# The first block's attention by token tile, with two heads on alternate partitions among zeros

## The chip, the cores and the metric

The kernel runs on one core of a Trainium2 chip. The metric is the device time of one execution in microseconds. Engines are PE (TensorE), DVE (VectorE), ACT (ScalarE), POOL (GpSimd) and SP (SyncE, which here only issues loads and stores). Each takes its instructions in the order of the program, and waits are on semaphores.

## The reference

4 batches of 768 tokens, 8 heads of 64. Attention is by chunks of 32 queries: each sees 8 memory rows and the keys from 16 ahead of the chunk to 8 behind it, 64 in all. The 3072 x 512 result goes through a rational function between two matrices, and then through a soft mixture of experts:

```python
scores = scale * np.matmul(q_c, k_full.transpose(0, 1, 3, 2))   # per chunk of 32 queries
a = np.exp(scores - max);  a = a / (a.sum() + 1e-9);  x = a @ v_full
h = x @ w_in                                                      # 512 -> 2048
P = a[0] + a[1]*h + a[2]*h**2 + a[3]*h**3
Q = 1.0 + abs(b[0])*abs(h) + abs(b[1])*h**2
y = (P / (Q + 1e-6)) @ w_out                                      # 2048 -> 512
logits = y @ phi      # soft mixture: softmax over tokens and over slots, 8 experts of 4 slots
```

w_in and w_out come as float64 and are narrowed to float32 on the chip.

## The kernel before

3072 tokens are worked off in six blocks of 512 (four token tiles of 128). A block has eight steps; step i makes 256 columns of h (`h_part`, L380: on PE, x turned times w_in), then the rational function (`a1`, L607 to L610 on ACT and L609 on DVE; `d1`, L619 and L620; `a2`, L624 and L625; `t`, L632 and L633), then `post` turns the result and adds its logits (L398, L405, L406). h has two buffers in PSUM, so h of the next step runs on PE while ACT and DVE work on this one.

Attention is a generator, `attention(pair)`, for two tiles at once. Its steps: scores (L168; 64 products of 64 x 32 x 64, a head and a chunk each, two heads on the two halves of the partitions), maximum and difference (L186, L189, DVE), exp (L190, ACT), transposes (L208, PE), copy (L212, ACT), sums and reciprocal (L197 to L199, DVE), the product with v (L228, 64 products), scaling (L238, DVE), transposes (L246, PE) and copy to x (L250, ACT). The pairs of the later blocks run in pieces (`at`) between the steps of the block before. The first block has none ahead of it: its two pairs A and B run at the start, in an order written out by hand in `KN['pre']`, one letter for the next piece of a generator (A, B; s, t and n narrow weights; c makes constants; fN are N idle products on PE, L288). That order is kept as it stands on PE, ACT, DVE and POOL. `KN['loads']` is the order of loads on SP; SP lets a load go when the eighth load before it has landed.

In block 0 the weights come in. For each step 1 MB of w_in (`load_w_in`, L317) and 1 MB of the turned w_out (`load_w_turned`, L323) go through four staging buffers `g`; `f64_narrow` makes float32 of them: L303 and L305 on ACT, L304 and L307 on DVE, for each of the two. `wp_sum` (L483 to L489) multiplies w_out by phi. `KN['ord0']` lists what step kk of block 0 issues: `s2` narrows w_in two steps ahead, `i4` loads it four ahead, `o3` loads the turned w_out three ahead, `n1` narrows it one ahead, `z0` multiplies it by phi. Within the steps a scheduler orders the instructions of an engine.

## Time and profile before

| | |
|---|---|
| median of 3 runs | 577.13 us (575.4 to 579.71) |
| the profiled execution | 577.91 us, span 575.8 us |
| busy of the span | PE 540.6 us (94%), DVE 456.3 (79%), ACT 427.9 (74%), POOL 122.2 (21%) |
| HBM | 94.44 MB read, 182 GB/s over the span |
| chain that ended last | PE 56%, DVE 15%, ACT 14%, DMA 8%, issue 4% |

The share of busy time is an average over stages with different limits: at the start the engines wait for loads and for each other, in block 0 the weights are narrowed beside the steps, later PE has three products for each of block 0's.

### The profile page before, as it was taken

The numbers are of one execution on the slowest core, as the hardware profiler recorded it, in microseconds if no ns is written. First come the engines' busy times: TensorE is split into PE (matmuls) and PEld (weight loads), VectorE is DVE, ScalarE is ACT, GpSimd is POOL, SyncE is SP. The second block draws the span as 40 slices with busy tenths as digits, with TensorE's granted clock in tenths as the row PEclk, the third lists the DMA queues.
The fourth block names the chain that finished last, engine by engine and source line by source line (L and its number), as shares of the span: only waits on it lengthen the run. The fifth ranks groups of instructions, "written<-read, shape, count | busy, mean of one in ns | idle before, by whom it ended". The sixth has DMA issues, their size and how long they took to land.

```text
span 575.8 us, 13647 instructions
## 1 busy us (share of the span) xinstructions
PE 540.6 (94%) x5874; PEld 362.1 (63%) x5874; DVE 456.3 (79%) x572; ACT 427.9 (74%) x551; POOL 122.2 (21%) x66
## 2 busy tenths in 40 slices
PE   6799897999999999999999999999999999999991
PEld 6644443557767767677766777776768767643351
DVE  3759988989898999979899799898898978831042
ACT  1489896897978999779787888896888978721132
POOL 0001111213221322313231313132223322300000
PEclk8799898999999999999999999999999999999996
DMA  8997854301125315341432335304349374799948
GB/s 319 361 382 256 279 189 162 137 12 56 56 76 183 129 56 183 115 170 36 161 111 74 114 107 184 110 12 174 110 145 372 106 252 150 268 392 410 409 173 357
DMA packets 28139, 105.80 MB, mean 184 GB/s; under 512 B 3376, under 2 KB 3504, under 8 KB 27056
## 3 DMA queue, kind: packets, MB, share of 16 engines
q1 hardware_dynamic: 26928, 100.74, 48.1%
q0 software_dynamic: 1152, 4.19, 1.8%
q8 instruction: 46, 0.75, 0.5%
q14 instruction: 13, 0.11, 0.0%
HBM read 94.44 MB, written 10.49 MB: 182 GB/s over the span
## 4 chain that ended last, share of the span: by engine, by line
PE 56%; DVE 15%; ACT 14%; DMA 8%; issue 4%; POOL 1%; ACTq 0%; SPq 0%; DVEq 0%; POOLq 0%
PE h L380 28%; DMA g<-in_w_turned_dram 5%; PE m L405 4%; PE m L458 4%; ACT S L607 3%; PE lg L398 3%; ACT S L608 3%; ACT g L406 3%; DVE T L619 3%; PE h L796 2%; PE m L228 2%; DVE T L620 2%; PE lg L833 2%; DMA g<-in_moe_w_in_dram 2%; DVE T L632 2%
## 5 line engine op out<-in xcount | busy, mean ns | idle before, releaser
L380 PE MATMUL h<-xt,win 128*128 128x512 f32 x1012 | 268.5, 414 | 0.7 <-DVE T L620 0.6
L380 PEld LDWEIGHTS h<-xt,win 128*128 128x128 f32 x1012 | 184.1, 188 | 50.9 <-issue 12.3
L585 POOL TENSOR_TENSOR S<-S,S 128x1024 f32<-128x1024 f32 x46 | 112.2, 2440 | 335.1 <-DVE S L609 282.1
L607 ACT ACTIVATE S<-h,ctab 128x1024 f32<-128x1024 f32 x47 | 52.5, 1117 | 38.3 <-PE h L380 37.5
L609 DVE SCALAR_TENSOR_TENSOR S<-S,S 128x1024 f32<-128x1024 f32 x47 | 57.3, 1220 | 24.3 <-ACT S L608 23.7
L619 DVE TENSOR_TENSOR T<-T,h 128x1024 f32<-128x1024 f32 x47 | 57.1, 1215 | 7.6 <-ACT T L610 7.6
L405 PEld LDWEIGHTS m<-ident,T 128*128 128x128 f32 x384 | 43.4, 141 | 29.4 <-issue 14.0
L620 DVE SCALAR_TENSOR_TENSOR T<-T,ctab,h 128x1024 f32<-128x1024 f32 x47 | 59.9, 1274 | 0.7
L632 DVE SCALAR_TENSOR_TENSOR T<-T,ctab,S 128x1024 f32<-128x1024 f32 x46 | 58.6, 1274 | 0.0
L633 DVE SCALAR_TENSOR_TENSOR T<-S,T 128x1024 f32<-128x1024 f32 x46 | 56.1, 1220 | 2.4 <-DVE T L632 0.5
L406 ACT ACTIVATE g<-m 128x512 f32<-128x512 f32 x96 | 53.2, 601 | 6.3 <-PE m L405 6.0
L610 ACT ACTIVATE T<-h,ctab 128x1024 f32<-128x1024 f32 x47 | 57.5, 1223 | 0.0
L625 ACT ACTIVATE S<-S,ctab 128x1024 f32<-128x1024 f32 x47 | 54.5, 1159 | 0.9
L624 ACT ACTIVATE S<-S 128x1024 f32<-128x1024 f32 x47 | 50.5, 1074 | 6.1 <-DVE S L609 6.1
L405 PE MATMUL m<-ident,T 128*128 128x128 f32 x384 | 53.0, 278 | 1.2 <-DVE a L189 1.2
L608 ACT ACTIVATE S<-h,ctab 128x1024 f32<-128x1024 f32 x47 | 52.7, 1121 | 0.9 <-DVE T L632 0.9
L380 PE MATMUL h<-xt,x 128*128 128x512 f32 x64 | 31.4, 621 | 3.6 <-DVE x L307 3.6
L398 PE MATMUL lg<-T,wp 128*32 128x512 f32 x192 | 33.1, 605 | 1.3 <-DVE T L633 0.7
L190 ACT ACTIVATE a<-a 128x512 f32<-128x512 f32 x22 | 13.4, 639 | 16.6 <-DVE a L189 16.6
L458 PE MATMUL m<-g,s 128*32 128x512 f32 x192 | 21.8, 595 | 0.4 <-ACT s L450 0.4
L303 ACT ACTIVATE g<-g 128x1024 uint32<-128x1024 uint32 x16 | 18.7, 1166 | 4.3 <-DMA g<-in_w_turned_dram 4.3
L380 PEld LDWEIGHTS h<-xt,x 128*128 128x128 f32 x64 | 11.2, 191 | 16.3 <-issue 15.1
(218 smaller groups left out, 673.5 us busy)
## 6 DMA issues: line engine op xcount, KB each, us to landing
win<-in_moe_w_dram SPq DMA_DIRECT2D x31, 512.0 KB, 7.3
k<-in_kw_dram SPq DMA_DIRECT2D x22, 512.0 KB, 6.3
v<-in_vw_dram SPq DMA_DIRECT2D x22, 512.0 KB, 5.2
g<-in_moe_w_in_dram SPq DMA_DIRECT2D x16, 512.0 KB, 7.3
g<-in_w_turned_dram SPq DMA_DIRECT2D x16, 512.0 KB, 6.5
x<-in_moe_w_out_dram SPq DMA_DIRECT2D x8, 1024.0 KB, 4.8
out_dram<-win SPq DMA_DIRECT2D x12, 512.0 KB, 5.0
q<-in_qw_dram SPq DMA_DIRECT2D x11, 512.0 KB, 3.8
```

The lines of the kernel that those rows point to most:

```text
L380: PE.matmul(tile_[f2] if step == total - 1 else tile_[:, f2, :], lhsT=ww[:, c, f2 * P:f2 * P + P], rhs=xx[:, c, :], start=(n == 0), stop=( ...
L405: st["turn"] = PE.transpose(pb[:, m, f2 * P:f2 * P + P], t_[:, f2, tt * P:tt * P + P], ident)
L406: ACT.activation(gts[b, qd][:, 2 * part:2 * part + 2, 2 * P * o:2 * P * o + 2 * P], pb, AF.Copy)
L585: POOL.tensor_tensor(out, q, w, ALU.mult)
L607: ACT.activation(s, hh, AF.Abs, scale=b0)
L608: ACT.activation(y, hh, AF.Square, scale=rb1)
L609: DVE.scalar_tensor_tensor(s, y, QC, s, ALU.add, ALU.add)
L610: ACT.activation(t, hh, AF.Identity, bias=a2, scale=a3)
L619: DVE.tensor_tensor(t, t, hh, ALU.mult)
L620: behind[kk] = DVE.scalar_tensor_tensor(t, t, a1, hh, ALU.add, ALU.mult).ins
L632: DVE.scalar_tensor_tensor(t, t, a0, w, ALU.add, ALU.mult)
L633: st["t"] = DVE.scalar_tensor_tensor(t, e, 2.0, t, ALU.subtract, ALU.mult, reverse0=True).ins
```

## The change

The attention of the first block is done by a new generator, `attention_first(n)`, one for each of the four token tiles (letters A to D). The two heads of a pair no longer stand on the two halves of the partitions: their rows of k and v go to alternate partitions, each head in its own half of a tile that is otherwise zero, so that one product of 128 rows by 128 columns gives a chunk of both heads; 16 products a tile where a pair had 64, for scores and for the product with v. The tiles of k and v are set to zero first, three by DVE and five by POOL; each is loaded by two loads of 64 rows. h of the first step is made in two halves of the columns (`h_first`, letters H and J), the first after two tiles. The orders of loads, of the start and of block 0 are new; the three loads of constants are one (`cst`, laid out on the host); the idle products have 256 columns.

```diff
 KN = {
-    'loads': "q0 q1 v0 i0 v1 c0 i1 o0 q2 v2 o1".split(),
-    'pre': "f10 A A f5 B B A A A A B B A A B B A A A A s B B B B A A f2 A B B A s A B B A f2 B s B B B c f4 t t n n".split(),
-    'pre2': "i2 o2 i3".split(),
-    'ord0': "at a1 z0 s2 h0 d1 at t o3 i4 n1 at a2 y h1 p0 at p1 at at".split(),
+    'loads': "Q0 Q1 K0 K1 V0 i0 K2 V1 K3 V2 V3 c0 i1 q2 i2 v2 o0 i3".split(),
+    'pre': "f4 A f1 B A B f1 A A f1 A C B B A A A B C B B B D C C f1 D D D s C C s C C H H D D D D J J c t t".split(),
+    'pre2': "".split(),
+    'ord0': "Z at a1 h0 d1 at s2 t i4 at a2 y n0 h1 p0 o1 at p1 at at".split(),
...
+    def load_first(kind, n):
+        if kind == "Q":
+            q_first[n] = (p_S("S", [P, HP, 2 * P]) if n else p_q("q", [P, HP, 2 * P]))
+            for par in range(2):
+                SP.dma_start(out=q_first[n][par:P:2], in_=qw[n, apart[par]])
+        else:
+            t, src = (k_first[n], kw[n // 2, :, n % 2]) if kind == "K" else (v_first[n], vwin[n // 2, :, n % 2])
+            for par in range(2):
+                SP.dma_start(out=t[par:P:2, par], in_=src[apart[par]])
+
+    def attention_first(n):
+        o = P * (n % 2)
+        sc = ps_h("h", [P, HP, 2, WIN])
+        for hp in range(HP):
+            for c in range(4):
+                PE.matmul(sc[CH * c:CH * c + CH, hp], lhsT=q_first[n // 2][:, hp, o + CH * c:o + CH * c + CH],
+                          rhs=k_first[n][:, :, hp, c, :], start=True, stop=True)
+        yield
...
+        DVE.tensor_reduce(mx, sc, AX.X, ALU.max)
+        pr = p_T("T", [P, HP, WIN, 2])
+        by = pr.rearrange("p h j a -> p h a j")
+        DVE.tensor_tensor(by, sc, mx.unsqueeze(3).to_broadcast([P, HP, 2, WIN]), ALU.subtract)
+        ACT.activation(pr, pr, AF.Exp, scale=SCALE)
+        yield
+        turned = bank([P, HP, P])
+        for hp in range(HP):
+            PE.transpose(turned[:, hp, :], pr[:, hp].rearrange("p j a -> p (j a)"), ident)
+        yield
+        pt = p_S("S", [P, HP, P])
+        ACT.activation(pt, turned, AF.Copy)
...
+        yield
+        pv = ps_h("h", [P, HP, 2, D])
+        for hp in range(HP):
+            for c in range(4):
+                PE.matmul(pv[CH * c:CH * c + CH, hp], lhsT=pt[:, hp, CH * c:CH * c + CH],
+                          rhs=v_first[n][:, :, c, hp, :], start=True, stop=True)
+        yield
+        x_tok = p_a4("a4", [P, HP, 2, D])
+        DVE.tensor_tensor(x_tok, pv, sm.unsqueeze(3).to_broadcast([P, HP, 2, D]), ALU.mult)
+        yield
...
+    def h_first(half):
+        if 0 not in hs:
+            hs[0] = ps_h("h", [P, 2, BLK])
+        o = slice(P // 2 * half, P // 2 * half + P // 2)
+        x = xt[0][0].rearrange("p c (t r) -> p c t r", t=TT)
+        for f2 in range(2):
+            to = hs[0][:, f2, :].rearrange("p (t r) -> p t r", t=TT)
+            for c in range(NC):
+                pins["PE"] = PE.matmul(to[:, :, o], lhsT=w_f[0][:, c, f2 * P:f2 * P + P], rhs=x[:, c, :, o],
+                                       start=(c == 0), stop=(c == NC - 1)).ins
             yield
...
+    for engine, ts in ((POOL, (v_first[0], v_first[1], k_first[3], v_first[2], v_first[3])), (DVE, (k_first[0], k_first[1], k_first[2]))):
+        for t in ts:
+            engine.memset(t.rearrange("p a h c j -> p (a h c j)"), 0.0)
...
-        SP.dma_start(out=ctab[:, 0:4], in_=ca.unsqueeze(0).to_broadcast([P, 4]))
-        SP.dma_start(out=ctab[:, 4:6], in_=cb.unsqueeze(0).to_broadcast([P, 2]))
-        SP.dma_start(out=u_acc[:, 0:NC * NSLOT], in_=phi)
+        SP.dma_start(out=u_all[:, BLK - NC * NSLOT:BLK + 6], in_=cst)
...
+            with tc.issue_after(pins[0]) if 0 in pins else nullcontext(), tc.issue_after(pins[1]) if 0 in pins else nullcontext():
+                for _ in {"s": narrow_w_in, "n": narrow_w_turned, "z": wp_sum, "i": load_w_in, "o": load_w_turned}[kind](n) or ():
+                    pass
...
-            DVE.scalar_tensor_tensor(s, y, QC, s, ALU.add, ALU.add)
-            ACT.activation(t, hh, AF.Identity, bias=a2, scale=a3)
+            pins[0] = DVE.scalar_tensor_tensor(s, y, QC, s, ALU.add, ALU.add).ins
+            pins[1] = ACT.activation(t, hh, AF.Identity, bias=a2, scale=a3).ins
```

`pins` makes DVE's and ACT's narrowing in a step of block 0 follow L609 and L610 of that step (new lines L660 and L661). Three places of the order follow; lines are those of each kernel's own file.

SP, from the first load on, before (q, k and xt hold q and k of the two pairs, v and S their v, g the weights):

```order
L133 DMA q_144<-in_qw_dram 128x1024
L135 DMA k_145<-in_kw_dram 128x1024 x2
L133 DMA xt_141<-in_qw_dram 128x1024
L135 DMA xt_142<-in_kw_dram 128x1024 x2
L143 DMA v_152<-in_vw_dram 128x1024 x2
L317 DMA g_155<-in_moe_w_in_dram 128x1024 x2
L143 DMA S_158<-in_vw_dram 128x1024
L143 DMA S_159<-in_vw_dram 128x1024
L270 DMA ctab_108<-in_moe_a_dram 128x4
L271 DMA ctab_108<-in_moe_b_dram 128x2
L272 DMA u_110<-in_moe_phi_dram 128x128
L317 DMA g_165<-in_moe_w_in_dram 128x1024 x2
```

and of the change (q and S hold q of two tiles each; k, xt_122, xt_124 and x_126 k of tiles 0 to 3; v, xt_123, x_125 and g_127 v of tiles 0 to 3):

```order
L251 DMA q_145<-in_qw_dram 64x1024 x2
L251 DMA S_148<-in_qw_dram 64x1024 x2
L255 DMA k_120<-in_kw_dram 64x1024 x2
L255 DMA v_121<-in_vw_dram 64x1024 x2
L255 DMA xt_122<-in_kw_dram 64x1024 x2
L384 DMA g_157<-in_moe_w_in_dram 128x1024 x2
L255 DMA xt_124<-in_kw_dram 64x1024 x2
L255 DMA xt_123<-in_vw_dram 64x1024 x2
L255 DMA x_126<-in_kw_dram 64x1024 x2
L255 DMA x_125<-in_vw_dram 64x1024 x2
L255 DMA g_127<-in_vw_dram 64x1024 x2
L339 DMA u_109<-in_cst_dram 128x134
```

All of q now comes first, each tile's k and v behind it in pairs of loads of 256 KB, and the constants in one load behind the last v.

PE, the end of the attention of block 0 and the first h, before (a and T hold exp or x of pairs A and B):

```order
L246 MATMUL m_538<-ident_106,a_3_460 128x128 x4
L288 MATMUL lg_547<-ident_106 128x128 x2
L246 MATMUL m_550<-ident_106,T_543 128x128 x4
L246 MATMUL m_556<-ident_106,T_543 128x128 x4
L288 MATMUL lg_569<-ident_106 128x128 x4
L380 MATMUL h_584<-xt_143,win_435 128x512 x8
```

and of the change, from the last product with v of tile 1 on (L262 scores, L279 transposes of exp, L291 product with v, L299 transposes of x, L316 half of h):

```order
L291 MATMUL h_311<-xt_123,S_297 32x128 x16
L299 MATMUL m_335<-ident_106,a_2_333 128x128 x4
L262 MATMUL h_341<-x_126,S_148 32x128 x16
L279 MATMUL m_358<-ident_106,T_330 128x128 x4
L355 MATMUL lg_369<-ident_106 128x256
L279 MATMUL m_376<-ident_106,T_373 128x128 x4
L291 MATMUL h_391<-x_125,S_363 32x128 x16
L299 MATMUL m_411<-ident_106,a_3_408 128x128 x4
L316 MATMUL h_417<-xt_119,win_387 128x4x64 x8
L291 MATMUL h_426<-g_127,S_381 32x128 x16
L299 MATMUL m_445<-ident_106,a_4_443 128x128 x4
L316 MATMUL h_417<-xt_119,win_387 128x4x64 x8
```

The scores of tile 3 (h_341) stand behind the last transposes of tile 1, and its product with v (h_426) behind the first half of h.

ACT, up to the first rational function, before (g_165 is w_in 1, g_168 and g_179 the turned w_out 0 and 1):

```order
L303 ACTIVATE g_165<-g_165 128x1024
L305 ACTIVATE g_165<-g_165 128x1024
L303 ACTIVATE g_168<-g_168 128x1024
L305 ACTIVATE g_168<-g_168 128x1024
L303 ACTIVATE g_179<-g_179 128x1024
L607 ACTIVATE S_638<-h_584,ctab_108 128x1024
```

and of the change (g_171 is w_in 1, g_179 w_in 2, g_185 the turned w_out 0; L658, L659 and L661 are L607, L608 and L610 of before, L370 and L372 are L303 and L305):

```order
L370 ACTIVATE g_171<-g_171 128x1024
L372 ACTIVATE g_171<-g_171 128x1024
L658 ACTIVATE S_508<-h_417,u_109 128x1024
L659 ACTIVATE S_510<-h_417,u_109 128x1024
L661 ACTIVATE T_509<-h_417,u_109 128x1024
L370 ACTIVATE g_179<-g_179 128x1024
L675 ACTIVATE S_571<-S_508 128x1024
L676 ACTIVATE S_571<-S_571,u_109 128x1024
L372 ACTIVATE g_179<-g_179 128x1024
L370 ACTIVATE g_185<-g_185 128x1024
L372 ACTIVATE g_185<-g_185 128x1024
```

Nothing of the turned w_out is narrowed ahead of the first rational function any more.

## Rows read from the trace of the kernel before

**Rows 1.** Busy by stretch: us; us busy (instructions) per engine; PEclk, DMA share, GB/s.

```profile
0.00:38.68 38.68, 30.25 (x678) 23.48 (x678) 21.35 (x53) 16.31 (x23) 0.75 (x7) 0.87 0.93 354
38.68:133.26 94.58, 86.13 (x772) 44.47 (x768) 85.41 (x95) 84.61 (x107) 18.39 (x7) 0.96 0.50 174
```

**Rows 2.** Chain that ended last, first 39 us: start, us, what.

```profile
6.88 11.52 DMA g<-in_moe_w_in_dram
...
18.42 8.85 DMA g<-in_w_turned_dram
...
27.30 10.18 DMA g<-in_w_turned_dram
```

**Rows 3.** Timeline of PE: start, us, line, operation, count [idle before <- what ended it].

```profile
8.21 1.30 PE L168 MATMUL h<-k,q 64*32 64x64 f32 x96 [0.75 <-DMA k<-in_kw_dram]
...
14.32 0.85 PE L168 MATMUL h<-xt,xt 64*32 64x64 f32 x64 [1.39 <-issue]
15.10 1.09 PE L208 MATMUL m<-ident,a 128*128 128x128 f32 x8
...
20.41 1.34 PE L228 MATMUL h<-v,a 64*32 64x64 f32 x72 [1.80 <-issue]
21.68 1.97 PE L208 MATMUL m<-ident,T 128*128 128x128 f32 x8
...
30.54 7.13 PE L380 MATMUL h<-xt,win 128*128 128x512 f32 x16
...
62.90 0.64 PE L483 MATMUL m<-win,u 128*32 128x256 f32 x8 [1.92 <-DVE win L307]
...
84.12 1.06 PE L398 MATMUL lg<-T,wp 128*32 128x512 f32 x8
...
97.66 1.92 PE L380 MATMUL h<-xt,x 128*128 128x512 f32 x2 [3.56 <-DVE x L307]
```

**Rows 4.** Timeline of SP, loads at their issue.

```profile
0.74 0.37 SPq L133 DMA_DIRECT2D q<-in_qw_dram  x1
...
14.59 0.33 SPq L272 DMA_DIRECT2D u<-in_moe_phi_dram  x1
...
21.17 0.33 SPq L133 DMA_DIRECT2D q<-in_qw_dram  x1
```

**Rows 5.** POOL's memset of L760: ns min/median/max, first and last start.

```profile
L760 POOL MEMSET wp<- x1: 528/528/528, 506.9 to 506.9; 128x512 f32 x1
```

**Rows 6.** Timeline of DVE at the start: difference, narrowing.

```profile
10.46 0.69 DVE L189 TENSOR_TENSOR a<-h,mx 128x512 f32<-128x512 f32 x1
...
19.89 0.66 DVE L304 TENSOR_SCALAR g<-g 128x1024 f32<-128x1024 f32 x1
...
23.66 1.22 DVE L307 SCALAR_TENSOR_TENSOR win<-g 128x1024 uint32<-128x1024 uint32 x1
```

**Rows 7.** Timeline of ACT: exp, narrowing and the first rational function, three waits.

```profile
11.19 0.63 ACT L190 ACTIVATE a<-a 128x512 f32<-128x512 f32 x1 [9.17 <-DVE a L189]
...
37.56 1.23 ACT L303 ACTIVATE g<-g 128x1024 uint32<-128x1024 uint32 x1 [0.85 <-DMA g<-in_w_turned_dram]
38.68 1.10 ACT L607 ACTIVATE S<-h,ctab 128x1024 f32<-128x1024 f32 x1
...
67.55 0.22 ACT L489 ACTIVATE wp<-m 128x64 f32<-128x64 f32 x1 [1.26 <-PE m L488]
...
90.88 1.18 ACT L303 ACTIVATE g<-g 128x1024 uint32<-128x1024 uint32 x1 [3.42 <-DMA g<-in_w_turned_dram]
...
100.47 0.60 ACT L406 ACTIVATE g<-m 128x512 f32<-128x512 f32 x1 [0.95 <-PE m L405]
...
133.26 1.12 ACT L607 ACTIVATE S<-h,ctab 128x1024 f32<-128x1024 f32 x1
```

**Rows 8.** Busy by stretch, as rows 1, from 20 to 40 us.

```profile
20.00:30.00 10.00, 9.19 (x236) 8.16 (x237) 6.02 (x12) 4.15 (x7) 0.00 (x0) 0.69 0.97 384
30.00:40.00 10.00, 10.00 (x98) 4.88 (x97) 4.99 (x9) 7.82 (x11) 0.00 (x0) 1.00 1.01 395
```

More of the change, by code (lines that the diff above doesn't have):

```diff
@@ L156, in attention @@
         qt, kt = ahead.pop(("q", pair))
[L157 to L161 removed]
+        sc = [bank([P, 2, HP, WIN]) for _ in range(2)]
         for n in range(2):
@@ L191, in attention @@
             yield
-        pt = tile4([P, 2, HP, P])
+        pt = p_a4("a4", [P, 2, HP, P])
         def sums():
@@ L213, in turns @@
             yield
-        for part in (turns, sums) if pair < 2 else (sums, turns):
-            yield from part()
+        yield from sums()
+        yield from turns()
         vt = ahead.pop(("v", pair))
-        if pair < 2:
-            both = ps_h("h", [P, 2, 2, HP, D])
-            pv = [both[:, par] for par in range(2)]
-        else:
-            pv = [bank([P, 2, HP, D]) for _ in range(2)]
+        pv = [bank([P, 2, HP, D]) for _ in range(2)]
         for n in range(2):
@@ new lines, in load_first @@
+    def load_first(kind, n):
[15 more added lines that the diff above has]
+        yield
+        s0 = (n % TPB) * P
+        if s0 == 0:
+            DVE.memset(sc[0:CH, :, :, 0:LEFT], NEG)
+        if s0 + P == S:
+            DVE.memset(sc[P - CH:P, :, :, CTX - RIGHT:CTX], NEG)
+        mx = p_sm("mx", [P, HP, 2], bufs=2)
+        DVE.tensor_reduce(mx, sc, AX.X, ALU.max)
[10 more added lines that the diff above has]
+        ACT.activation(pt, turned, AF.Copy)
+        sm = p_sm("sm", [P, HP, 2], bufs=4)
+        DVE.tensor_reduce(sm, by, AX.X, ALU.add)
+        DVE.tensor_scalar(sm, sm, 1e-9, None, ALU.add)
+        DVE.reciprocal(sm, sm)
+        yield
[7 more added lines that the diff above has]
+        DVE.tensor_tensor(x_tok, pv, sm.unsqueeze(3).to_broadcast([P, HP, 2, D]), ALU.mult)
+        yield
+        pb = bank([P, HP, P])
+        for hp in range(HP):
+            PE.transpose(pb[:, hp, :], x_tok[:, hp].rearrange("p a d -> p (a d)"), ident)
+        yield
+        o = (P // TT) * n
+        to = xt[0][0].rearrange("p h (t r) -> p h t r", t=TT)[:, :, :, o:o + P // TT]
+        ACT.activation(to, pb.rearrange("p h (r t) -> p h t r", t=TT), AF.Copy)
+        yield
```

119 lines of the change are left out of this document (50 added, 69 removed).

## The prediction

> **What bounds the kernel now.** The diff ends in the first of six blocks, so three stretches are read first [rows 1]. Up to 38.68 us, where the rational function of the first step begins (L607 on h [rows 7]), the DMA engines are 93% busy and ACT 16.31 of 38.68 us. From there to 133.26 us, the first L607 of the second block, the eight steps of block 0 run: PE 86.13, DVE 85.41 and ACT 84.61 of 94.58 us, DMA at 0.50. Three engines are near full at once; ACT idles 9.97 us. Behind that instant the order of instructions is the same in both kernels, but for a few rows at the start of the second block. So two instants carry the forecast: the start of the first L607 (S, now 38.68) and of the ninth (E, now 133.26). E moves one for one into the time, because the work behind it stays.
>
> The chain that ended last runs through loads of weights from 6.88 to 37.48 us [rows 2]. Those loads are not all that holds the start up, though. The first h products begin at 30.54 and take 7.13 us [rows 3]; before them PE stands for 1.39 and 1.80 us on "issue", waiting for nothing that the profile shows. The w_in weights of step 0 landed at 18.40 us already. The start is a chain of handoffs through PE, DVE and ACT beside the loads; block 0 is a matter of three nearly full engines.
>
> **Loads.** The half tiles carry the same bytes as before. The old 0.5 MB loads land in a row: the third lets PE go on at 8.21 [rows 3]; L272 waits for the seventh and goes at 14.59, L133 for the twelfth at 21.17 [rows 4], and the tenth lands at 18.40 [rows 2], 1.27 to 1.38 us apiece behind the seventh. In the new order K of tiles 0 to 3 is third, fifth, eighth, tenth, and the last V twelfth: 8.2, 10.7, 15.9, 18.4 and 21.1 us. (The eighth is taken at 14.59 + 1.27, the fifth at 8.21 + 2 x 1.27.) Three small loads of constants become one ahead of w_in 1, which pays nothing, since w_in 1 is needed only at 37 us.
>
> Whether 64 rows to every second partition move as fast no row shows. Bounds: the same rate, or half of it (eight such units stand ahead of K of tile 3: 18.4 + 8 x 1.27 = 28.6 us). I take the same rate, nearest to every row. The Trainium skill ("SBUF — State Buffer", Door 1: the DMA port swizzle) says that the rate depends on how many ports the partitions reach: 196 GB/s for 64 neighbouring ones against 328 for all 128. By its table alternate partitions reach all the ports, so it would leave the sum as it is; no run here shows either.
>
> **Zeros.** A 128x2048 memset is not in the trace. For POOL L760 gives 0.53 us for 512 columns [rows 5], so 2.1 us, five in a row from 1.4 to 11.9 us. For DVE: between 1.4 (twice L304's 0.66) and 2.4 us (twice L307's 1.22) [rows 6]; I take 2.1, so 2.8, 4.9 and 7.0 us. They gate loads: K of tile 0 would be issued at 2.3 us (four issues of 0.37 from 0.74 on [rows 4]) and goes at 2.8, while the 1 MB of q ahead of it moves till nearly 7 (1.27 before the third load); K of tile 2 waits till 7.0, while the loads ahead of it move till 14.6. I cost the zeros at nothing; without that cover they cost 0.5 us on the path.
>
> **The start by hand.** Sixteen products of a tile are four rounds of four on four column groups. Lower bound: 4 x 0.21 + 0.2 = 1.05 us, since four products of 256 columns take 0.64 and of 512 columns 1.06 us [rows 3]. Upper bound at half the clock: 4 x 0.43 + 0.2 = 1.9. The old products took 0.85 us for a tile (x64 in the row at 14.32), so fewer instructions are no gain of PE time; I take 1.25. Eight transposes took 1.09 and, at 21.68 us, 1.97 us [rows 3]: four are 0.55 to 1.0, taken 0.7. DVE: maximum, difference and scaling 0.69 each, sums as long and 0.3 for two small instructions behind them (an estimate); ACT: exp 0.63, copies 0.60 (as L406's), narrowing 1.18 each (L303 at 90.88) and 0.05 less with overlap, then DVE's 1.22 [rows 6, 7]. With 0.05 us per handoff, in the order of the program: scores of tile 0 at 8.2; tile 1 at 10.75; pt of tile 0 at 14.1, behind the exp of tile 1; tile 2 at 16.0; tile 1's last transpose ends at 21.4, and only then, by PE's order, the scores of tile 3, though its K landed at 18.4. Difference done 24.1, exp 24.8, pt 26.2, then the conversion of w_in 0 to 29.75. The first half of h, half of 7.13, runs to 33.4; behind it PV of tile 3, scaling, transposes, copy to 36.75; the second half ends at 40.4 = S. All lower bounds give 38.5, all upper bounds (with the first half of h at 5.4) 48. So half of h early does not bring S forward: **+1.7 us**.
>
> **What moves into block 0.** Before S, ACT now converts w_in 0, w_in 1, w_turned 0 and half of w_turned 1, the last (L303) at 37.56 [rows 7]; in the change only w_in 0 and 1, as the order of ACT shows. Three instructions of 1.18 us, less 0.1 each for the overlap of neighbours (L303 at 37.56 takes 1.23, L607 starts 1.12 later), join block 0: **+3.2 us** of ACT, 2.4 of DVE. Both engines have some 9 us free there, but the three nearly full engines wait for each other, so I count the ACT figure in full.
>
> **What block 0 gets back.** Three of ACT's waits hang on weights that came late: 3.42 us for a load of w_turned (L303 at 90.88), 1.26 us (L489 at 67.55) behind PE's 1.92 us wait for a converted weight, 0.95 us (L406 at 100.47) behind PE's 3.56 us wait at 97.66 for L307 [rows 3, 7]. The change loads w_in earlier, w_turned one step ahead, and binds the conversions behind the step's rational function. By SP's order a load is issued a step or more ahead (94.58 / 8 = 11.8 us) and lands 8.85 to 10.18 us after its issue where the queue is full [rows 2]. I take all three as gone: **-5.6 us**. If none goes: 0.
>
> Sum: 577.91 (the profiled execution: span 575.8 and 2.1 around it) + 1.7 + 3.2 - 5.6 = 577.2. The median of the runs is 0.8 lower, 577.13, so 576.4; I say 576.5. Differences of about 1% (5.8 us) are what a measurement of this kernel can tell from no change.
>
> **Rivals.**
> Faster: PE's order does not hold tile 3 back. If its scores start when K lands at 18.4 and everything runs at the lower bounds, 18.0 us of chain follow: S = 36.4. With ACT's work of 84.6 + 3.2 and 3 us of idling E is 127.2, 6.1 earlier: 571 us. For it: the two "issue" waits of 3.2 us stood between far more PE instructions than the new start has. Against it: the four lines of work share one PE order. 0.27.
>
> Slower: PE's clock. The granted clock was 0.69 between 20 and 30 us [rows 8], a mean over both levels (1.2 and 2.4 GHz), and the same eight transposes took 1.09 and 1.97 us. The new start has pauses between its products, and h is split in two with a pause between. At the upper bounds S = 48: 577.9 + 9.3 + 3.2 - 5.6 = 584.8, by the median 584. It decides from S = 47 on. For it: the halved speed stands on PE's rows; against: PE is at work some 17 of the 21 us from 8 to 29 in the chain above. 0.13. The Trainium skill ("TensorE: Matmul & The Clock Gate", Part 1) says that the throttled state is the default and that activity releases it. That speaks against a sparser start, and the trace agrees in that the clock is 1.00 from 30 us on, under dense products; by the rule alone the sum would be the 584 of this rival.
>
> Slower, by loads: half rate puts K of tile 3 at 28.6; from there 19.0 us of the chain above follow (40.4 less 21.4), so S = 47.6 and the time 583, by the median. 0.05. Loads or conversions of w_turned take the place of the stalls, since they now trail: nothing comes back, 582, and from there over 1% with S past 41.3. 0.12, half of it over the limit. The forecast itself, with the start anywhere from 38.5 to 43: 0.43.
>
> **Numbers.** Faster by over 1%: the first rival, 0.27. Slower: 0.13 + 0.05 + 0.06 = 0.24. Within 1%: 0.49. The range runs from 567 (the faster rival with no idling at all in block 0 is 568) to 585, just past the slower one; the forecast's own is 574 to 580 (S from 38.5 to 43).
>
> **What would show it.** The first rational instruction (new L658) at 40.4 us; scores of tile 3 at about 21.4, after K landed at 18.4; 69 KB of constants landing within 1 us; the memsets done at 7.0 and 11.9; block 0 from S to the ninth L658 92.2 us long (94.58 + 3.2 - 5.6), with no ACT wait over 1.5 us for a load. I am wrong in the start if K of tile 3 lands after 21.4, or if sixteen products take 1.9 us; wrong in block 0 if ACT idles still 10 us there or less than 3.

## The result and the profile after

The change makes the kernel slower by 1.1%: 584.36 us against 577.3 (medians, measured side by side), ratio 1.0112 with a 95% interval of 1.0093 to 1.0131. The forecast was 576.5 and "within 1%"; 584.36 lies inside the wide range and outside the forecast's own 574 to 580.

The profiled execution of the after takes 584.1 us with a span of 582.2, that of before 577.91 with 575.8. The after's, cut at the first rational function (S, 41.91), the ninth (E, 135.67), the twelfth, the 16th and the 47th (all L658), columns as in [rows 1]:

```profile
0.00:41.91 41.91, 28.84 (x348) 21.64 (x356) 22.09 (x40) 12.91 (x20) 9.47 (x12) 0.92 0.87 316
41.91:135.67 93.76, 87.94 (x843) 45.35 (x843) 88.52 (x99) 88.22 (x108) 17.57 (x7) 1.00 0.53 180
135.67:167.49 31.82, 28.34 (x385) 20.64 (x387) 28.83 (x37) 25.07 (x34) 7.17 (x3) 0.95 0.22 73
41.91:205.45 163.54, 153.84 (x1674) 93.26 (x1674) 151.92 (x176) 145.65 (x181) 34.36 (x14) 0.99 0.43 146
205.45:490.22 284.77, 281.95 (x2948) 205.04 (x2945) 253.13 (x294) 238.43 (x298) 79.50 (x39) 1.00 0.39 136
490.22:582.20 91.98, 75.12 (x653) 40.33 (x649) 34.00 (x55) 30.97 (x53) 6.75 (x6) 0.94 0.83 325
```

The same stretches of before, as far as [rows 1] do not have them:

```profile
133.26:162.95 29.69, 29.69 (x394) 21.60 (x390) 27.71 (x36) 25.25 (x34) 7.22 (x3) 1.00 0.23 75
38.68:200.92 162.24, 153.38 (x1610) 93.40 (x1603) 148.08 (x172) 142.23 (x179) 35.26 (x14) 0.98 0.42 144
200.92:485.24 284.32, 281.60 (x2948) 205.01 (x2945) 252.92 (x294) 238.40 (x298) 79.48 (x39) 1.00 0.39 136
485.24:575.80 90.56, 75.33 (x653) 40.23 (x649) 34.00 (x55) 30.97 (x53) 6.75 (x6) 0.94 0.84 330
```

Read down the differences: the start +3.23 us, block 0 (93.76 for 94.58 [rows 1]) -0.82, from the ninth to the twelfth rational function +2.13, from there to the 16th nothing (37.96 for 37.97), to the 47th +0.45, the tail +1.42. E moved by 2.41 us only. So in this pair of executions 4.0 of the 6.4 us lie behind E, where the forecast had nothing; how much of that holds over several executions is worked out below.

The start on PE, columns as in [rows 3] (L262 scores, L316 half of h, L291 the product with v):

```profile
9.45 1.94 PE L262 MATMUL h<-k,q 128*32 128x128 f32 x32 [4.31 <-DMA k<-in_kw_dram]
...
12.83 1.94 PE L262 MATMUL h<-xt,q 128*32 128x128 f32 x32 [0.29 <-DMA xt<-in_kw_dram]
...
18.36 1.08 PE L262 MATMUL h<-xt,S 128*32 128x128 f32 x32
...
22.65 0.66 PE L299 MATMUL m<-ident,a 128*128 128x128 f32 x4 [0.81 <-DVE a L295]
23.24 1.08 PE L262 MATMUL h<-x,S 128*32 128x128 f32 x32
...
31.29 3.69 PE L316 MATMUL h<-xt,win 128*128 128x256 f32 x16 [1.64 <-DVE win L374]
34.92 1.08 PE L291 MATMUL h<-g,S 128*32 128x128 f32 x32
...
38.15 3.72 PE L316 MATMUL h<-xt,win 128*128 128x256 f32 x16 [0.69 <-ACT xt L303]
```

The scores of tile 1, at 12.83 us, wait for their K. Those of tile 3 run at 23.24 us, behind transposes of tile 1 that wait for DVE, long after their K has come (19.09 in the trace). The first half of h waits for DVE's half of the narrowing of w_in 0 (L374).

### The profile page after: what moved, and what is told of

It reads as the page before. It is cut to its first block, busy times and chain, and to the rows that moved or that the text cites. A ratio compares the mean times of both kernels' runs of the same rounds, so it can differ in the third digit from the quotient of the medians.

```text
span 582.2 us, 13128 instructions
## 1 busy us (share of the span) xinstructions
PE 539.8 (93%) x5604; PEld 360.3 (62%) x5604; DVE 461.1 (79%) x562; ACT 428.0 (74%) x551; POOL 130.1 (22%) x71
## 4 chain that ended last, share of the span: by engine, by line
PE 51%; ACT 18%; DVE 18%; issue 4%; DMA 4%; POOL 2%; SPq 1%; ACTq 0%; DVEq 0%; POOLq 0%
PE h L447 24%; PE m L525 4%; ACT g L473 3%; ACT S L658 3%; ACT S L659 3%; DVE T L670 3%; PE m L472 3%; PE m L214 3%; PE h L850 2%; PE lg L465 2%; DVE T L671 2%; PE lg L887 2%; DVE T L683 2%; DVE S L660 2%; ACT g L372 2%
## 5 line engine op out<-in xcount | busy, mean ns | idle before, releaser
L447 PE MATMUL h<-xt,win 128*128 128x512 f32 x996 | 261.1, 411 | 5.0 <-ACT win L406 3.9
L447 PEld LDWEIGHTS h<-xt,win 128*128 128x128 f32 x996 | 181.3, 189 | 54.4 <-issue 9.7
L658 ACT ACTIVATE S<-h,u 128x1024 f32<-128x1024 f32 x47 | 52.5, 1116 | 37.7 <-PE h L447 34.8
L660 DVE SCALAR_TENSOR_TENSOR S<-S,S 128x1024 f32<-128x1024 f32 x47 | 57.3, 1219 | 24.1 <-ACT S L659 23.7
L671 DVE SCALAR_TENSOR_TENSOR T<-T,u,h 128x1024 f32<-128x1024 f32 x47 | 59.8, 1273 | 0.7
L683 DVE SCALAR_TENSOR_TENSOR T<-T,u,S 128x1024 f32<-128x1024 f32 x46 | 58.5, 1273 | 0.0
L661 ACT ACTIVATE T<-h,u 128x1024 f32<-128x1024 f32 x47 | 57.5, 1224 | 0.0
L676 ACT ACTIVATE S<-S,u 128x1024 f32<-128x1024 f32 x47 | 54.3, 1156 | 0.9
L659 ACT ACTIVATE S<-h,u 128x1024 f32<-128x1024 f32 x47 | 52.7, 1121 | 0.6 <-DVE T L683 0.6
L372 ACT ACTIVATE g<-g 128x1024 f32<-128x1024 f32 x16 | 18.6, 1161 | 4.1 <-DVE g L371 4.1
L214 PE MATMUL m<-v,a 64*32 64x64 f32 x1280 | 18.7, 223 | 2.2 <-ACT a L202 1.6
L214 PEld LDWEIGHTS m<-v,a 64*32 64x32 f32 x1280 | 15.6, 105 | 5.8 <-ACT a L202 2.0
```

The lines of the kernel that those rows point to most:

```text
L447: PE.matmul(tile_[f2] if step == total - 1 else tile_[:, f2, :], lhsT=ww[:, c, f2 * P:f2 * P + P], rhs=xx[:, c, :], start=(n == 0), stop=( ...
L658: ACT.activation(s, hh, AF.Abs, scale=b0)
L659: ACT.activation(y, hh, AF.Square, scale=rb1)
L660: pins[0] = DVE.scalar_tensor_tensor(s, y, QC, s, ALU.add, ALU.add).ins
L661: pins[1] = ACT.activation(t, hh, AF.Identity, bias=a2, scale=a3).ins
L671: behind[kk] = DVE.scalar_tensor_tensor(t, t, a1, hh, ALU.add, ALU.mult).ins
```

## The experiments

Each number below is from the kernel's own profiled execution: S; from S to the 16th rational function; from there to the 47th; the tail behind it. Then the median and its ratio to the kernel before on the same chip. "Early" kernels share a start that narrows w_in 0 earlier (below).

| kernel | S | to 16th | to 47th | tail | median | ratio (95%) |
|---|---|---|---|---|---|---|
| before | 38.68 | 162.24 | 284.32 | 90.56 | 577.3 | |
| after | 41.91 | 163.54 | 284.77 | 91.98 | 584.36 | 1.0112 (1.0093 to 1.0131) |
| e1_order | 43.48 | 164.38 | 284.77 | 92.57 | 583.31 | 1.0108 (1.0066 to 1.0151) |
| e2_before_row | 38.71 | 161.07 | 284.37 | 90.45 | 577.84 | 1.0002 (0.998 to 1.0025) |
| e3_start | 37.16 | 165.81 | 284.97 | 91.36 | 581.06 | 1.0055 (1.0035 to 1.0075) |
| e5_q_single | 42.76 | 161.48 | 284.75 | 91.91 | 583.02 | 1.0086 (1.0059 to 1.0112) |
| e6_whole | 43.45 | 161.56 | 286.62 | 91.67 | 585.23 | 1.012 (1.0093 to 1.0147) |
| e7_before_whole | 38.33 | 160.66 | 286.54 | 90.47 | 578.92 | 1.003 (1.0013 to 1.0048) |
| e8_best | 37.63 | 165.96 | 286.48 | 92.23 | 581.9 | 1.0074 (1.0048 to 1.01) |
| e11_split | 38.93 | 162.90 | 284.37 | 90.40 | 579.17 | 1.0016 (0.9996 to 1.0035) |
| e12_moved | 39.30 | 163.60 | 284.43 | 90.37 | 578.7 | 1.0018 (0.9999 to 1.0036) |
| e13_back | 39.64 | 161.51 | 284.72 | 92.13 | 581.22 | 1.006 (1.0036 to 1.0083) |
| e14_late | 39.70 | 167.76 | 284.41 | 90.33 | 583.14 | 1.0092 (1.0062 to 1.0122) |
| e15_shift | 47.65 | 167.49 | 284.67 | 90.99 | 588.08 | 1.0208 (1.0177 to 1.0238) |
| e16_back_shift | 42.40 | 165.46 | 284.75 | 90.39 | 584.84 | 1.0136 (1.0114 to 1.0159) |
| e17_shift12 | 43.70 | 165.02 | 284.87 | 90.41 | 586.69 | 1.0137 (1.0105 to 1.017) |
| e18_back_shift12 | 40.55 | 161.76 | 284.35 | 90.54 | 578.47 | 0.9997 (0.9977 to 1.0017) |
| e19_early | 36.73 | 162.69 | 284.81 | 90.77 | 575.74 | 0.9968 (0.9947 to 0.9988) |
| e20_early_no_shift | 37.42 | 160.93 | 284.77 | 91.78 | 576.69 | 0.9987 (0.9969 to 1.0005) |

Two executions of the same instructions differ. Before and e2 are alike up to the tenth step, yet their first three steps take 35.64 and 33.95 us (the two rows, of before and of e2): the granted clock is 0.95 in the first and 1.00 in the second, and ACT is equally busy.

```profile
38.68:74.32 35.64, 32.21 (x327) 15.72 (x320) 31.93 (x38) 33.53 (x42) 5.08 (x2) 0.95 0.76 269
```
```profile
38.71:72.66 33.95, 31.07 (x356) 15.45 (x342) 31.79 (x39) 33.52 (x42) 5.08 (x2) 1.00 0.82 281
```

A single stretch is thus good to about 2 us.

### An instruction of ACT behind block 0: it does not carry the loss

In the after's second block, ACT takes the rational function of the tenth step ahead of the split of a weight (L406), and PE then stands for that split. ACT and then PE of the after:

```profile
151.83 1.11 ACT L658 ACTIVATE S<-h,u 128x1024 f32<-128x1024 f32 x1 [1.47 <-POOL S L635]
152.84 1.14 ACT L676 ACTIVATE S<-S,u 128x1024 f32<-128x1024 f32 x1
153.88 1.04 ACT L406 ACTIVATE win<-win 128x1024 fp32r<-128x1024 f32 x1
```
```profile
154.98 3.02 PE L447 MATMUL h<-xt,win 128*128 128x512 f32 x7 [3.26 <-ACT win L406]
```

e1 puts the split first in the after; e2 puts it behind in before.

```diff
-        ACT.activation(wh, f, AF.Copy)
+        st["split"] = ACT.activation(wh, f, AF.Copy).ins
...
-            ACT.activation(s, hh, AF.Abs, scale=b0)
+            with tc.issue_after(st["split"]) if kk == NSTEP + 2 else nullcontext():
+                ACT.activation(s, hh, AF.Abs, scale=b0)
```

> The changed kernel with one constraint more: the first rational instruction of step 10 on ScalarE is issued behind the exponential and the weight split of step 9, as it was before the change. Theory: that one row ahead of the split made TensorE wait 3.26 us for the split weights and then run at the lower clock, so that step 10 to step 11 took 15.7 us instead of 9.9. It then expects step 10 to 11 at about 10 us, no TensorE wait over 1 us for the split there, and a median of 579 us (578 to 580). Rival: the time comes from the start that is 3.2 us later and carried on through, and the row only showed it; then step 11 starts at 167 us again and the median stays at 584.

> The kernel before with only that row moved: the first rational instruction of step 10 on ScalarE is issued ahead of the exponential and the weight split of step 9, everything of the start as it was. Theory: step 10 to 11 grows from 9.9 to about 15.5 us, TensorE waits about 3 us for the split and then shows the lower clock for some us, and the median is 582 (580 to 584). Rival: without the later start the row costs only its own 1 us and the median is 577 to 578.

PE of e1, and of e2:

```profile
157.05 1.90 PE L447 MATMUL h<-xt,win 128*128 128x512 f32 x7 [0.81 <-ACT win L406]
```
```profile
151.12 1.88 PE L380 MATMUL h<-xt,win 128*128 128x512 f32 x7 [1.23 <-ACT win L339]
```

The wait of 3.26 us falls to 0.81 in e1, yet the median does not come down beyond its interval (1.0108); in e2 the order of the after costs nothing (1.0002). The theory, 5 us from this row, falls: the wait was visible, but it does not carry the loss. A part is not excluded, since the lower end of e1's interval lies 2.7 us under the after's ratio; in the traces the stretch from the ninth to the twelfth function is 31.82 us in the after and 28.83 in e1.

### The start

e3 moves both letters s, which narrow w_in 0, far ahead in the order of the start, and takes tile 3 up to its product with v ahead of the first half of h. e5 (on top of e1) loads q with one load of 128 rows in place of two of 64.

```diff
-    'pre': "... A A f1 A C B B A A A B C B B B D C C f1 D D D s C C s C C H H D D D D J J c t t".split(),
+    'pre': "... A A f1 s A C B B A s A A B C B B B D C C f1 D D D C C D C C D H D D H J J c t t".split(),
```
```diff
-            for par in range(2):
-                SP.dma_start(out=q_first[n][par:P:2], in_=qw[n, apart[par]])
+            SP.dma_start(out=q_first[n], in_=qw[n])
```

> The changed kernel with another order of the same instructions at the start: the first weight tile is narrowed as soon as it has landed (about 15 us instead of 27.7 us), the score products of tile 3 are not behind the transposes of tile 1, and the products of tile 3 with the values stand ahead of the first half of h. The scheduler then puts the row of step 10 behind the split by itself. Theory: ninth and first rational instructions hang on the order at the start, not on the loads: the first one starts at 37 us instead of 41.9, and with the row mended the median is 574 (572 to 577). Rival: the first block takes back what the start gains, as it took back 0.8 us of what it lost, or the loads end at 41 us anyhow (the changed kernel's w_in 1 landed at 41.3): then only the row's share is gained and the median is 578 to 579.

> e1 with the queries of the first two pairs laid out in memory as they are to stand on the partitions, so that each is one load of 128 rows instead of two of 64; the keys and values are loaded as before. Theory: a load of 64 rows costs SyncE's queue 0.6 us of issuing where one of 128 rows costs 0.37 to 0.45, so the first scores start at about 8.2 us instead of 9.45, but the first rational instruction is held by the order of work on ScalarE and TensorE and moves by less than 0.5 us; the median stays within 0.3% of e1. Rival: the ladder of loads sets the start, and both the first rational instruction and the median move 1.2 us.

Against e1, on which it is built, e5's first scores begin at 7.58 us for 8.96, and S comes 0.72 us earlier (42.76 for 43.48); the medians do not tell the two apart. Its load of constants also goes out earlier, at 4.26 us for 17.15. So the issue of q's loads carries 0.7 us of the late start and not all of it: tile 1's scores still wait for their K, until 12.36 us. e3 brings S to 37.16, yet only from 1.0112 to 1.0055: its stretch to the 16th step is 165.81, with that of e8, which is built on it, the longest of those without a delay or short idle products. What swallows the gain is the next question but one.

e14 delays the start of before: three further copies of the first ACT instruction, with block 0's narrowing bound as in the change.

```diff
-            ACT.activation(s, hh, AF.Abs, scale=b0)
+            for _ in range(4 if kk == 0 else 1):
+                ACT.activation(s, hh, AF.Abs, scale=b0)
```

> The kernel before with its first rational instruction run four times in place (the same values to the same tile), and no narrowing drawn ahead of it, so that all that follows on ScalarE starts 3.0 us later; the start and its loads stay as they were. Theory: a later start of the first block goes one for one into the time: 580.8 us (580 to 581.5). Rival: the block's waits for loads and weights (10 us on ScalarE) take up most of it: 578 to 579.

```profile
39.70 4.56 ACT L611 ACTIVATE S<-h,ctab 128x1024 f32<-128x1024 f32 x4 [1.00 <-PE h L380]
44.16 1.11 ACT L612 ACTIVATE S<-h,ctab 128x1024 f32<-128x1024 f32 x1
```

The second instruction starts at 44.16 instead of 39.7, 4.46 us later, and the median is 0.92% (5.3 us, interval 3.6 to 7.0) up. The binding of the narrowing is in that too; e12 below, which has it as well, stands at 0.18%. A late start is thus paid about one for one; block 0 does not take it up.

### Halves of the logits and their order: not the cause

A step's logits are four products on four column groups, and where PE's order puts two of them apart, such a half takes as long as the whole: L398 of before takes 1.05 us at 93.06 for a half, 1.06 at 84.12 [rows 3] for a whole. In blocks 0 to 5 the order of the after has 32 pieces where before has 30. e11 gives before 32; e6, e7 and e8 (the after, before, e3) order the tiles so that there are 28.

```diff
-                for j in range(4):
+                for j in (2, 3, 0, 1):
```
```diff
-                for j in range(4):
+                for j in range(2 if b == 0 else 0, 4):
...
+        elif o == 0 and b == 0:
+            for j in range(2):
+                PE.matmul(st["lg"][32 * j:32 * j + 32, :], lhsT=wp[:, 4 * qd + j, :], ...)
```

> The changed kernel with the four products of a logit set issued in the order 2, 3, 0, 1, so that the set can't start before its second half is ready; the planner then keeps the sets whole (28 pieces in the program instead of 32) and also puts the row of step 10 behind the weight split by itself. Theory: each split set costs TensorE, which is never idle there, about 1 us (in the changed kernel's trace a half set takes 1.05 us and a whole one 1.06), so that mending four splits and the row gives back 4 to 6 us: 579 us (578 to 580.5), with step 8 to step 15 at 66 to 67 us. Rival: the loss is the later start alone; then whole sets change nothing and the median stays at 583 to 584.

> The kernel before with the same order 2, 3, 0, 1 of the four products of a logit set: 28 pieces instead of 30. Theory: two splits of 1 us each are saved, 575.7 us (575 to 576.7). Rival: whole sets wait for their second half and hold up what stands behind them on TensorE; then 577.5 or more.

> The changed kernel with the start of e3_start and whole logit sets (28 pieces instead of the 34 of e3_start). Theory: 6 splits of 1 us come back, so that 581.1 becomes 575 us (574 to 576.5), 2 us below the kernel before, with the first rational instruction at 37.2 us. Rival: what e3_start lost behind its early start is a wait that has nothing to do with the sets; then 580 to 581.

> The kernel before with the logit sets of the first block issued in two halves on purpose, the first half one step earlier, as the planner issued them in the changed kernel: 32 pieces instead of 30, everything else as before. Theory: two more splits cost 2 us, 579.8 us (579 to 580.5). Rival: the halves fill gaps of TensorE in the first block (it idles 5 us there) and cost nothing: 577.5 to 578.

e7, from the 16th to the 47th:

```profile
198.99:485.53 286.54, 280.58 (x2948) 205.58 (x2945) 253.00 (x294) 238.54 (x298) 79.48 (x39) 1.00 0.39 135
```

PE's busy time falls by 1.0 us against before (280.58 for 281.60) and the stretch grows by 2.2: the whole set waits for its later half. Two more pieces (e11) cost 0.16%, with zero in the interval. This falls too.

### The narrowing that was moved

e12 moves the narrowing, with its loads, its binding and the product with phi, in before: w_turned 0 and 1 leave the start and trail in block 0. e13 does the reverse on e3: w_turned 0 goes back, ahead of the first rational function. e20 lets it go back without delaying that function: its two halves stand between the letters of tiles 2 and 3, and its load goes ahead. The diffs are shortened to the lines on the order. The first diff is e12 against before, the second e13 against e3, the third e20 against e13.

```diff
-    'pre': "... B s B B B c f4 t t n n".split(),
-    'ord0': "at a1 z0 s2 h0 d1 at t o3 i4 n1 at a2 y h1 p0 at p1 at at".split(),
+    'pre': "... B s B B B c f4 t t".split(),
+    'ord0': "Z at a1 h0 d1 at s2 t i4 at a2 y n0 h1 p0 o1 at p1 at at".split(),
```
```diff
-    'pre': "... D H D D H J J c t t".split(),
-    'ord0': "Z at a1 h0 d1 at s2 t i4 at a2 y n0 h1 p0 o1 at p1 at at".split(),
+    'pre': "... D H D D H J J c t t n n".split(),
+    'ord0': "z0 at a1 h0 d1 at s2 t i4 at a2 y n1 h1 p0 o2 at p1 at at".split(),
```
```diff
-    'loads': "... V3 c0 i1 q2 i2 v2 o0 i3".split(),
-    'pre': "... D D D C C D C C D H D D H J J c t t n n".split(),
+    'loads': "... V3 c0 o0 i1 q2 v2 i2 i3".split(),
+    'pre': "... D D D C C D n C C D n H D D H J J c t t".split(),
```

> The kernel before with its own start (two pairs, as it was), but with the narrowing planned as in the changed kernel: the first tile of w_turned and the first half of the third of w_in are narrowed behind the first rational step instead of ahead of it, every tile of w_turned one step later, and its sum of products too. Theory: these 3.5 us of ScalarE and 3.8 us of VectorE take the place of the 10 us in which ScalarE waited in the first block, the last tile of w_turned is summed in step 8 (about 139 us) instead of step 7 (130 us), and what the first rational instruction gains (about 1 us, 37.7) is lost again: 579 us (578 to 581). Rival: the moved work is hidden in the waits and the gain of the start stays: 576.5.

> e3_start with that work taken back to where it was before the change: the first tile of w_turned narrowed ahead of the first rational instruction, each later tile and its sum one step earlier. Theory: the first rational instruction at 38 to 39 us, the last sum in step 7, TensorE without its 2 to 3 us wait for it in step 8, median 578 us (577 to 580), level with the kernel before. Rival: the rest of the loss of e3_start sits elsewhere and the median stays at 581.

> e19_early without the short products, so that the last block of TensorE's instructions falls among the stores again. Theory: tail 92 instead of 90.5 us, median 1.5 us over that of e19_early. Rival: the shift doesn't count in the median, the two are level.

e12's ACT where before waited 3.42 us for this load [rows 7], and e3's PE at the end of block 0:

```profile
93.03 1.20 ACT L303 ACTIVATE g<-g 128x1024 uint32<-128x1024 uint32 x1 [0.20 <-DMA g<-in_w_turned_dram]
```
```profile
140.68 0.76 PE L555 MATMUL m<-stack,s 128*128 128x32 f32 x4 [2.07 <-ACT s L552]
```

In before the moved work goes into the wait (3.42 to 0.20 us) and costs 0.18% (0 to 0.36). On the new loads, where that wait is gone already, it costs 0.68%, 3.9 us, with the changed order of loads in it: from e3 (1.0055) to e20 (0.9987), at nearly one S (37.16, 37.42). It also makes the last product with phi trail into step 8, where PE waits 2.07 us. e13's order delays S by 2.5 us against e3, as the narrowing stands ahead of it, and gives back 4.3 behind it; the medians of the two are level (1.0055, 1.006).

### The tail: PE's own instructions among the stores

The order of the tail is the same in all kernels. Its length falls in two groups: 90.33 to 90.56 us in the six executions with before's start, 91.36 to 92.57 in the eight with a new start and no short idle products. Before, after (pages):

```profile
PE 540.6 (94%) x5874; PEld 362.1 (63%) x5874; DVE 456.3 (79%) x572; ACT 427.9 (74%) x551; POOL 122.2 (21%) x66
```
```profile
PE 539.8 (93%) x5604; PEld 360.3 (62%) x5604; DVE 461.1 (79%) x562; ACT 428.0 (74%) x551; POOL 130.1 (22%) x71
```

PE's instructions come in blocks over the DMA engines, q8 in the DMA queues: with 270 fewer of them, and as many fewer weight loads, the blocks are 44 for 46. The last block then falls elsewhere: in the after at 563 us, 73 us behind the 47th step, when the output's stores begin; in before at 70 or 71, ahead of them. Stores of the after, us by us, columns as in [rows 1]; and the queue's row of 563 to 564:

```profile
563.00:564.00 1.00, 1.00 (x18) 0.94 (x15) 1.00 (x3) 1.00 (x3) 0.00 (x0) 1.00 0.74 270
...
566.00:567.00 1.00, 1.00 (x17) 0.97 (x13) 1.00 (x2) 1.00 (x3) 0.00 (x0) 1.00 0.55 221
```
```profile
q8 instruction: 1, 0.02, 10.8%
```

SP shows what is held up: the issue of the third of the twelve output stores, of the after and of before:

```profile
563.76 2.25 SPq L926 DMA_DIRECT2D out_dram<-win  x1
```
```profile
558.96 0.40 SPq L872 DMA_DIRECT2D out_dram<-win  x1
```

It starts just behind the block (563.6 in the trace). In seven of the eight long tails this issue takes 1.88 to 2.25 us, in e20 the fourth store's takes 1.50; in the other executions of the table the two take 0.39 to 0.40 and 1.02 to 1.05.

24 or 12 short idle products at the start (128 x 32, in place of two of the wide ones) move that block without touching the tail: 24 in e15 (the after) and e16 (e13), 12 in e17 (the after) and e18 (e13).

```diff
-    'pre': "f4 A f1 B A B ...".split(),
+    'pre': "f2 g24 A f1 B A B ...".split(),
...
+        elif what[0] == "g":
+            t = ps_l("lg", [P, 2, P])
+            for _ in range(int(what[1:])):
+                PE.matmul(t[:, 0, 0:32], lhsT=ident, rhs=ident[:, 0:32], start=True, stop=True)
```

> The changed kernel with TensorE's instruction stream some 90 instructions longer at its very start: half of the first idle products replaced by 24 short ones (128x32), while TensorE waits for the first keys anyway; the order of everything else is as in the changed kernel. Theory: TensorE fetches its instructions in blocks over its own DMA queue; with half as many products its stream got shorter, so that the last block's transfer now falls among the output stores, whose rate then drops from 400 to 221 GB/s for a microsecond, and the tail behind the last rational step is 91.4 to 92.6 us instead of 90.3 to 90.6. Shifted by 90 instructions the block lands before the stores: tail 90.4 us, median 583 us. Rival: the tail is longer for another reason, and stays at 92 us; median 584.4.

> e13_back with the same shift of TensorE's stream. Theory: tail 90.4 us instead of 92.1, median 579.7 us. Rival: tail 92 us, median 581.

> e15_shift with 12 short products instead of 24: in e15_shift the 48 instructions of the 24 took 10.45 us and drove the start back by 4 us, so that its time said nothing of the tail. Twelve take 5.2 us and end at about 8.7 us, before the first keys (9.45 us). Theory: the last block of TensorE's instructions comes some 3 us earlier than in the changed kernel, ahead of the stores; tail 90.4 to 91 us instead of 92.0, first rational instruction at 42 to 43.5 us as in the changed kernel, median 583 us (582 to 584). Rival: the tail's 1.5 us are in the trace only, or come back elsewhere: 584.4 or more.

> e13_back with the same 12 short products. Theory: tail 90.4 to 91 us instead of 92.1, median 579.7 us (578.5 to 581). Rival: 581.2 or more.

e16's stores, in the us in which the after has 221 GB/s, and its tail:

```profile
566.00:567.00 1.00, 1.00 (x19) 0.97 (x16) 1.00 (x3) 1.00 (x3) 0.00 (x0) 1.00 1.00 406
...
492.61:583.00 90.39, 75.21 (x653) 40.22 (x649) 34.01 (x55) 30.93 (x53) 6.76 (x6) 0.95 0.84 330
```

In these four the block falls 66 to 71 us behind the 47th step, and the tails are 90.39 to 90.99; e19's, below, is 90.77. But the idle products cost more than they bring where many stand at the start: e15's take 10.45 us and S goes to 47.65; in medians only e18 gains (1.006 to 0.9997, 3.6 us, more than the tail has to give). e17 gains nothing, its S being 43.70. So the traces show a tail longer by about 1.4 us where the block falls among the stores, and SP held up in the issue of a store there. Why a block holds it no row shows, and the medians do not settle what it is worth.

### Together: a version that beats both

e19 is e18 with the loads and the place of the narrowing as in e20.

> e18_back_shift12 with the first tile of w_turned loaded right behind the last V (ahead of q, k and v of the third pair and of the third tile of w_in) and narrowed ahead of the last copies of tiles 2 and 3: in e18_back_shift12 ScalarE waited 3.27 us for it at 38.5 us, while h was ready at 36.6. Theory: the first rational instruction at 36.6 us instead of 40.6, with the narrowing where it was before the change and the tail short; an earlier start counts one for one, as the later one did, so 574.5 us (573.5 to 577). Rival: what the start gains is lost in the first block, as in e3_start: 578.

```profile
0.00:36.73 36.73, 31.15 (x360) 25.19 (x364) 24.27 (x42) 15.36 (x23) 9.47 (x12) 1.00 0.93 338
36.73:199.42 162.69, 157.28 (x1678) 95.12 (x1677) 146.50 (x172) 143.36 (x178) 34.13 (x14) 0.97 0.44 151
199.42:484.23 284.81, 281.69 (x2943) 204.74 (x2941) 253.38 (x295) 238.47 (x299) 79.47 (x39) 1.00 0.39 137
484.23:575.00 90.77, 75.35 (x653) 40.22 (x649) 34.01 (x55) 30.94 (x53) 6.75 (x6) 0.96 0.85 329
```

575.74 us, 0.9968 (0.9947 to 0.9988) of before, and by the two ratios about 1.4% under the after. S is 5.2 us earlier than in the after, and e20, without the idle products, has 4.5 of that. The clock of 1.00 in the first row says nothing of the idle products: e19 has no record of the clock before 14.3 us, and its sixteen products take 1.94 and 1.93 us at 8.75 and 12.34, as in the after at a granted 0.50. The interval of e20 (0.9969 to 1.0005) overlaps that of e19, so what the short tail adds stays open.

## Why the prediction was wrong

**The step that failed** is "I take all three as gone: -5.6 us", with which idle time returned to ACT was counted in full into the time. Two more went wrong: "E moves one for one into the time, because the work behind it stays", and S, which came out too small.

Four executions with the after's start and order (after, e1, e5, e6) stand against four with before's (before, e2, e7, e11); the small edits of these kernels are in the numbers. The means differ by 4.2 us in S, 0.6 in block 0, 0.4 from there to the 16th step, 0.3 to the 47th and 1.6 in the tail. That is 7.15 us together, where the medians differ by 7.1. The forecast had 1.7, -2.4 and nothing behind E.

**Returned stalls, -5.6: mis-sized, the largest term.** The ACT waits went as forecast (none over 1.5 us for a load in block 0), and ACT idles 5.5 us there (93.76 less 88.22) where it idled 9.97. But block 0, which with the moved work was to be 2.4 us shorter, is 0.8 shorter in the profiled pair, before and after, and 0.6 longer in the means. The four lie from 93.33 to 96.72 and from 92.63 to 95.16, so the sign is not settled, but a gain of 2.4 did not come. ACT's idle time is what the pace of PE leaves it: e1 has the same instructions in block 0 as the after, in the same order, and with the granted clock at 0.96 for 1.00 its block 0 is 2.96 us longer, with ACT no busier (88.48 for 88.22) and idle for 8.24 us.

```profile
43.48:140.20 96.72, 90.87 (x843) 46.33 (x843) 88.56 (x99) 88.48 (x108) 17.59 (x7) 0.96 0.51 175
```

The two rows of before and e2 above say the same. PE's own idle time from S to the 16th step did not fall by 5.6: it is 6.8 to 11.5 us in the four with the new start and 8.0 to 9.4 in before's four, of which before and e2 lack the records of some products and so read too high. The sign that the forecast set for block 0 (ACT idle for 10 us, or for less than 3) did not show this, as it looks at ACT.

**E one for one: wrong for the tail, open for the rest.** In the profiled pair, before and after, E moves 2.41 of 6.4 us; in the means it moves 4.9, and the 16th step 5.3. E is read on ACT, and ACT had slack there. Before's next rational function:

```profile
143.38 1.12 ACT L607 ACTIVATE S<-h,ctab 128x1024 f32<-128x1024 f32 x1 [2.86 <-PE h L380]
```

ACT waits 2.86 us for PE, and PE is busy 29.69 of the 29.69 us behind E. So the end of block 0 is better read where PE is paced again, at the 16th step. The work behind E stays in order but not in its meeting with the DMA engines: the tail is 1.4 us longer in the pair, and it was put at nothing.

**Moved work, +3.2: right in size, by another route.** ACT's busy time in block 0 rose by 3.6 us (88.22 for 84.61), DVE's by 3.1. e3 to e20 prices it at 3.9 us; but half of that stands in e3's trace as PE's wait of 2.07 us for the last product with phi, which the forecast did not have, so the agreement is in part luck. e12 prices it at 1.0, since there it lies in waits that before still has. The forecast took both, full cost and full return, and the second was not to be had.

**S, +1.7: too small.** It is 3.2 in the profiled execution, 4.1 to 4.8 in e5, e6 and e1. The scores of tile 1 run at 12.83 us for 10.75, those of tile 3 at 23.24 for 21.4, and the first half of h at 31.29 for 29.75, which is the whole miss in the after. From tile 1 to tile 3 the chain is no longer than forecast; it starts late, because the loads came late: K of tile 0 landed at 9.32 us for 8.2, of tile 1 at 12.70 for 10.7, of tile 3 at 19.09 for 18.4. The rows of 5 to 10 us, of before, the after and e5:

```profile
5.00:10.00 5.00, 3.14 (x135) 2.65 (x135) 0.37 (x2) 0.00 (x0) 0.00 (x0) 0.91 0.98 384
```
```profile
5.00:10.00 5.00, 0.69 (x13) 0.58 (x16) 2.59 (x6) 0.00 (x0) 5.00 (x4) 0.86 0.79 229
```
```profile
5.00:10.00 5.00, 3.17 (x35) 2.01 (x34) 3.50 (x9) 0.00 (x0) 5.00 (x4) 1.00 0.85 309
```

In the first 10 us the after's loads move 0.85 MB less than before's (156 for 172 GB/s in the first 5), some 2 us at 400 GB/s. e5, with q in whole loads, has part of that back; what holds the rest no run separates. The products of 1.94 us, which the forecast named as a sign of being wrong, did come, at 9.45 and 12.83.

In e1, e5 and e6 the first half of h takes 5.25 to 5.38 us for 3.69, with the granted clock at the lower level for part of it. The half in e1, then e1 and the after by stretch:

```profile
31.30 5.25 PE L316 MATMUL h<-xt,win 128*128 128x256 f32 x16 [1.66 <-DVE win L374]
```
```profile
28.00:31.00 3.00, 0.83 (x12) 0.42 (x4) 1.98 (x3) 2.38 (x3) 0.00 (x0) 1.00 1.02 412
31.00:36.50 5.50, 5.20 (x19) 4.09 (x19) 0.16 (x1) 0.00 (x0) 0.00 (x0) 0.69 0.82 282
```
```profile
31.00:36.50 5.50, 4.70 (x48) 3.77 (x48) 0.58 (x2) 0.00 (x0) 0.00 (x0) 1.00 0.87 293
```

In e1 PE is busy 0.83 of 3 us, then the clock granted is 0.69, a mean of 1.2 and 2.4 GHz. In the after PE is busy 0.84 of the same 3 us, and the clock stays at 1.00. The Trainium skill ("TensorE: Matmul & The Clock Gate", Part 1) has throttling as the default that activity releases; the fall in e1 agrees, and the after has the same pause without it.

**The rivals.** "PE's clock" had 584 as its time, but with S at 48; the clock was worth 1.6 us on S in some executions, so that the number is a coincidence. Nearest in its numbers is the last rival, "nothing comes back, 582, and from there over 1% with S past 41.3", at a chance of 0.12; not its mechanism, since no load or conversion of w_turned holds ACT for over 1.5 us in block 0.

**Right:** the mechanism of the start (PE's order holds tile 3 back; half of h early brings nothing forward), the zeros (done at 7.28 on DVE and 10.0 on POOL, and no wait of the after's start goes back to them; the slow issue of q hides them, for in e5 K of tile 0 goes out at 3.03 us, behind DVE's zeros, done at 3.01), and, from 10 us on, the rate of alternate partitions: DMA share and GB/s stay at before's level (0.97 and 384 in [rows 8]), as this row of the after shows (from 15 to 20 us, where almost only half loads land, it is 411 GB/s):

```profile
10.00:15.00 5.00, 4.71 (x63) 3.25 (x56) 1.73 (x4) 0.63 (x1) 0.08 (x2) 0.50 1.02 416
```

By its table of ports the Trainium skill ("SBUF — State Buffer", Door 1) would have it so, and this row agrees; the lower rate from 5 to 10 us it leaves unexplained.

**What stays open:** the 0.4 us between the 16th step and the 47th, and why e3 takes 4.9 us longer than e20 from S to the 16th step, 4.1 of it behind the ninth; the 2.07 us wait of PE is half of that.

## What to carry to other kernels

A wait that goes is worth what the pacing engine gets of it: count the idle time of the engine that sets the pace, not that of the engine on which the wait is seen, and read a stretch's end where that engine is paced. Work moved into waits is free only while the waits are there, so a change that moves work and removes the waits cannot be credited with both. Compare the same stretch in several executions before a difference of 2 us is given a cause: here the profiled pair alone puts most of the loss behind block 0, and the means of four put most of it in the start.
